# One core: the same 773 operations of an attention and token-mixing kernel in a newly solved order

## The chip, the cores and the metric

The kernel runs on one core of a Trainium2 chip. The metric is the device time of one execution in microseconds (us), the median of several runs.

## What is computed

Eight sequences of 576 tokens go through sliding-window attention with linear biases (8 heads of 64, window 128) and then, as 512 channels, through a token-mixing block. Inputs and output are fp32.

```python
scores = scale * np.matmul(q, k.transpose(0, 1, 3, 2))
mask = (rel >= 0) & (rel < window)
scores = np.where(mask, scores + bias[None], -1000000000.0)
attn = softmax(scores)
x = np.matmul(attn, v)                      # then heads side by side: [8, 576, 512]
...
wq = x @ w_q; wk = x @ w_k                  # 512 -> 64
W_tok = scale * np.einsum('bsd,btd->bst', wq, wk)
mixed = np.einsum('bst,btd->bsd', W_tok, x)
out = np.maximum(mixed, 0.0) @ w_out
```

## The kernel before

The kernel is built of 773 named operations. Each is declared once with `add` (its name, what it waits for, what it emits) and then emitted in the order of one long string, `ORDER`. One word of it is `name:engine`, and for TensorE also a PSUM place and a number of fillers:

```python
for word in ORDER.split():
    name, eng, *rest = word.split(":")
    ...
        op.bank = tuple(int(c) for c in rest[0])
        op.fill = int(rest[1]) if len(rest) > 1 else 0
```

Engines are P (TensorE), A (ScalarE), V (VectorE), G (GpSimd) and S (SyncE). Each engine runs its own words strictly in the order of the string, and waits at a word until what it depends on is done. PSUM is four pairs of banks; `:2` takes pair 2, `:21` its second bank. An operation that writes a place waits until the place's last content was evicted. `TW0.0:P:0:12` runs twelve products of a zero tile (fillers) ahead of TW0.0; they keep TensorE busy and compute nothing.

The names, with the batch as the first number:

- Loads, all issued by GpSimd: Lq, Lk, Lv and Lt (the last 64 tokens of q or k), Lwq, Lwk, Lwo (the weights). They cast fp32 to 16 bits. FQ0 and FQ1 load the first queries through SyncE, and CQ0 and CQ1 cast them. For batches 0 to 3 a q or k load takes four heads at once (256 KB in the tile); for batches 4 to 7 it takes 128 tokens (128 KB), like a v load.
- Constants: zerop, pads, zeros, ones0 to ones4 (memsets), iota, dist, mask, ident, idh, perm, bias, biasl.
- Attention: TW, TN and TT transpose q and k on TensorE (line 217), and ETW, ETN and ETT evict them. QK makes the scores of one block of keys and four heads, EXP evicts them with an exponential (ScalarE, line 604), MUL multiplies by the exponentiated bias and mask (VectorE, line 611). PV multiplies with v; its output also carries the row sums. X divides by them (VectorE, lines 649 and 650).
- Mixing: XT transposes x and EXT evicts it; WQ and WK are the two projections, G multiplies the second by x, MX mixes the tokens, RM is the relu, OUT the last product. EWQ, EWK, EG and EO evict. DO stores a block of 128 tokens, on GpSimd or SyncE.

All products go through one helper (line 214) and all loads through another (line 220), stores through line 223, so the profile's lines are those of helpers.

Loads are paced in the order in which they are emitted: each has a price in us, and a load waits until so many before it have landed that at most `AHEAD = 6.0` us of loads are under way. HOLD takes note of a load (the fourth from the end); the first SyncE store emitted behind HOLD waits for it. Stores emitted before HOLD do not wait for loads.

An eviction may run on ScalarE or VectorE; EXP is always ScalarE's, MUL and X always VectorE's.

Of the kernel before, what the change touches and what calls it, by code (L numbers as in the profile page):

```python
# [45 lines left out]
X0.0:V ETW1.1.0:A Lv0.4:G PV0.2:P:1 ETW1.1.1:A Lk2.1:G MUL0.3.0:V PV0.1:P:2 EXP0.3.1:A  # L46
X0.2:V Lk2.0:G QK1.2.1:P:0 EXP1.2.1:A QK1.1.1:P:3 MUL0.3.1:V Lq2.1:G TW1.0:P:1:1 X0.1:V
EXP1.1.1:A Lq2.0:G PV0.3:P:0 ETW1.0.0:A MUL1.1.1:V Lwq:G QK1.3.1:P:2 ETW1.0.1:A X0.3:V
PV0.4:P:3 EXP1.3.1:A QK1.0.1:P:1 X0.4:V Lv1.0:G XT0.0:P:0 EXP1.0.1:A EXT0.0:V Lv1.1:G
XT0.2:P:20:2 QK1.2.0:P:3 QK1.0.0:P:1 EXT0.2:A MUL1.0.1:V EXP1.2.0:A XT0.1:P:0 Lwk:G  # L50
QK1.1.0:P:2 MUL1.3.1:V EXP1.0.0:A EXT0.1:V Lv1.2:G TW2.1:P:3 MUL1.2.0:V EXP1.1.0:A Lv1.3:G
MUL1.2.1:V QK1.3.0:P:0 ETW2.1.1:A TW2.0:P:1 MUL1.0.0:V Lt1.2:G ETW2.1.0:A wqq:V EXP1.3.0:A
Lv1.4:G MUL1.1.0:V WQ0.0:P:20 ETW2.0.0:V PV1.0:P:3 Lt1.3:G ETW2.0.1:A WQ0.1:P:21 X1.0:V
EWQ0.0:A Lt1.1:G QK2.1.1:P:0 EWQ0.1:A QK2.0.0:P:1 Lwo.0:G PV1.1:P:2 MUL1.3.0:V EXP2.0.0:A
WK0:P:30 Lt1.0:G X1.1:V EXP2.1.1:A WQ0.2:P:31 PV1.2:P:1 Lk3.0:G EWQ0.2:V QK2.1.0:P:2 EWK0:A
ones4:G X1.2:V PV1.3:P:0 EXP2.1.0:A QK2.0.1:P:3 Lq3.0:G X1.3:V PV1.4:P:1 EXP2.0.1:A
# [6 lines left out]
RM1.1:V Lv2.3:G PV2.0:P:0 RM1.3:A ETW3.0.0:V OUT0.0:P:20 RM1.2:A X2.0:V Lq4.0:G EO0.1:A
OUT0.2:P:10 EO0.0:A MUL2.1.0:V QK3.0.0:P:3 MUL2.3.1:V Lq4.1:G QK3.1.0:P:0 EO0.2:A PV2.1:P:2
MUL2.3.0:V EXP3.0.0:A Lv3.0:G OUT1.0:P:11 X2.1:V EXP3.1.0:A Lq4.2:G PV2.2:P:3 MUL3.0.0:V
TW3.1:P:2 EO1.0:A Lk4.3:G MUL3.1.0:V X2.2:V QK3.2.0:P:0 ETW3.1.0:A Lk4.1:G PV2.4:P:1
EXP3.2.0:A ETW3.1.1:V OUT0.3:P:20 Lk4.0:G X2.4:V QK3.2.1:P:3 Lk4.2:G QK3.0.1:P:0 EO0.3:V
EXP3.2.1:A PV2.3:P:1 Lq4.3:G OUT1.3:P:21 EXP3.0.1:A X2.3:V Lv3.1:G WQ1.2:P:20 QK3.3.1:P:3
EWQ1.2:A EO1.3:V QK3.3.0:P:1 EXP3.3.1:A XT2.1:P:0 Lt2.3:G MUL3.2.1:V OUT1.2:P:20 Lv3.2:G
EXP3.3.0:A EXT2.1:V XT2.2:P:21 XT2.0:P:3 MUL3.0.1:V TN4.0.0:P:0 Lv3.4:G EXT2.2:A EXT2.0:A  # L70
MX1.2:P:1 WQ2.1:P:21 ETN4.0.0:V Lv3.3:G RM1.4:A QK3.1.1:P:3 MUL3.2.0:V EWQ2.1:A TN4.1.0:P:1
EXP3.1.1:A PV3.0:P:0 Lt2.0:G MUL3.3.1:V OUT1.4:P:21 Lv4.0:G X3.0:V ETN4.1.0:A TN4.0.1:P:3
EO1.2:A TN4.1.1:P:1 MUL3.1.1:V Lq5.3:G QK4.0.1:P:0 ETN4.0.1:A WK2:P:20 EO1.4:V ETN4.1.1:A
Lt2.2:G PV3.1:P:3 EXP4.0.1:A MUL3.3.0:V Lq5.2:G QK4.0.0:P:1 X3.1:V WQ2.0:P:21 EXP4.0.0:A
# [6 lines left out]
MUL4.1.1:V OUT2.1:P:21 Lq6.1:G X4.0:V ETN5.0.0:A Lk6.0:G TN5.1.0:P:0 EO2.3:A XT3.1:P:3
MUL4.3.0:V ETN5.1.0:A QK4.3.1:P:1 OUT2.2:P:20 Lv5.0:G EXP4.3.1:A EXT3.1:V MUL4.2.1:V Lt3.0:G
QK5.0.0:P:0 EO2.1:A QK5.0.1:P:3 MUL4.3.1:V EXP5.0.0:A PV4.1:P:1 Lk5.2:G EO2.2:V WK3:P:21
EXP5.0.1:A Lv5.1:G X4.1:V PV4.2:P:0 WQ3.1:P:20 Lk6.1:G EWK3:A X4.2:V QK5.1.0:P:3 EWQ3.1:A
QK5.1.1:P:1 EXP5.1.0:A PV4.3:P:2 Lv5.2:G MUL5.0.1:V PV4.4:P:0 EXP5.1.1:A X4.3:V Lq6.2:G
WQ2.2:P:30 G3:P:31 X4.4:V EWQ2.2:A Lq6.0:G XT4.1:P:2 EG3:A XT4.0:P:1 EXT4.1:A TN5.1.1:P:3
EXT4.0:V Lq7.0:G MX3.1:P:0 ETN5.1.1:A MX3.0:P:2 RM3.3:V OUT2.0:P:10 RM3.2:A Lk6.3:G RM3.1:V
RM3.0:A XT4.2:P:11 TN6.1.0:P:3 Lt3.2:G MUL5.0.0:V QK5.3.0:P:0 EXT4.2:A EO2.0:A QK5.3.1:P:2
ETN6.1.0:V Lv5.3:G OUT3.0:P:11 EXP5.3.1:A MUL5.1.1:V Lq6.3:G PV5.0:P:3 EXP5.3.0:A MUL5.1.0:V
OUT3.2:P:10 Lt3.1:G X5.0:V EO3.0:A WK4:P:20 Lk6.2:G EO3.2:A MUL5.3.1:V QK5.2.1:P:0  # L90
TN6.0.0:P:3 EWK4:A MX2.2:P:1 EXP5.2.1:A Lt3.3:G OUT3.1:P:21 ETN6.0.0:V Lk7.0:G RM2.4:V
PV5.1:P:3 MUL5.2.1:V EO3.1:A QK6.0.1:P:0 Lq7.1:G QK5.2.0:P:1 X5.1:V EXP6.0.1:A G4:P:20
Lv5.4:G MUL5.3.0:V WQ3.2:P:21 WQ4.0:P:30 EXP5.2.0:A Lk7.1:G EWQ3.2:V WQ4.1:P:31 EG4:V
EWQ4.0:V MX3.2:P:0 TN6.0.1:P:2 EWQ4.1:A Lk7.3:G TN6.1.1:P:1 RM3.4:V ETN6.0.1:A XT5.0:P:3
ETN6.1.1:V TT3:P:0 Lv6.2:G EXT5.0:A QK6.1.1:P:2 MUL5.2.0:V MX4.0:P:1 ETT6:A MX4.1:P:3
EXP6.1.1:A Lv7.3:G RM4.0:V OUT3.4:P:00 RM4.1:V RM4.3:A Lv6.1:G PV5.3:P:2 RM4.2:A MUL6.0.1:V
QK6.0.0:P:3 EO3.4:A Lv6.0:G PV5.2:P:1 X5.3:V ETT7:A OUT4.2:P:00 EXP6.0.0:A Lq7.2:G X5.2:V
QK6.1.0:P:2 Lq7.3:G QK6.2.1:P:3 MUL6.0.0:V EXP6.1.0:A TN7.1.0:P:1 OUT4.3:P:01 EO4.2:V
DO3.4:G EXP6.2.1:A ETN7.1.0:V PV5.4:P:2 MUL6.1.1:V QK6.3.0:P:1 EO4.3:A Lk7.2:G TN7.0.0:P:3
X5.4:V EXP6.3.0:A OUT4.1:P:00 Lv6.3:G MUL6.1.0:V ETN7.0.0:A QK6.3.1:P:2 XT5.1:P:1 MUL6.3.0:V  # L100
DO0.0:G EXP6.3.1:A QK6.2.0:P:3 OUT3.3:P:01 EO4.1:V Lv7.1:G EXT5.1:A MUL6.2.1:V PV6.0:P:2
EXP6.2.0:A DO2.2:G OUT4.0:P:00 X6.0:V Lv6.4:G EO3.3:A WQ5.1:P:10 MUL6.2.0:V EO4.0:A DO0.1:G
XT5.2:P:11 TN7.0.1:P:3 TN7.1.1:P:2 EWQ5.1:A EXT5.2:V QK7.0.0:P:0 ETN7.0.1:V DO2.3:G
ETN7.1.1:A PV6.2:P:1 MUL6.3.1:V EXP7.0.0:A DO1.0:G WQ5.0:P:30 X6.2:V PV6.1:P:2 Lv7.4:G
# [2 lines left out]
DO0.3:G QK7.3.1:P:3 X6.3:V G5:P:20 EXP7.3.1:A DO4.2:G XT6.0:P:0 EG5:V DO1.2:G XT6.1:P:1
EXT6.0:A XT6.2:P:21 QK7.0.1:P:3 EXT6.1:V EXT6.2:A Lv7.2:G EXP7.0.1:A MX5.1:P:0 MX4.2:P:2
WQ6.0:P:10 RM5.3:V DO3.0:G WK6:P:11 RM5.1:A MUL7.3.1:V RM4.4:A WQ5.2:P:30 DO1.4:G
QK7.2.1:P:0 EWQ5.2:A MUL7.0.0:V MX5.0:P:2 EWK6:A QK7.3.0:P:3 EWQ6.0:V RM5.0:A G6:P:11  # L110
RM5.2:V DO3.2:G EXP7.3.0:A WQ6.1:P:10 MUL7.1.0:V DO2.0:G OUT5.2:P:20 EG6:A EWQ6.1:V
EXP7.2.1:A MUL7.1.1:V OUT5.3:P:21 MUL7.3.0:V EO5.2:A MX6.1:P:1 MUL7.2.0:V MX5.2:P:3
MX6.0:P:0 EO5.3:A OUT5.1:P:20 RM5.4:V RM6.1:A MUL7.0.1:V RM6.3:A PV7.4:P:3 MUL7.2.1:V
RM6.2:A PV7.1:P:1 EO5.1:A X7.4:V OUT5.0:P:21 RM6.0:A DO5.1:G X7.1:V PV7.0:P:3 PV7.3:P:0
EO5.0:A X7.0:V WQ6.2:P:20 PV7.2:P:1 DO5.0:S OUT6.2:P:21 X7.3:V DO2.1:S OUT6.1:P:30 DO1.3:S
X7.2:V EO6.2:A EWQ6.2:A XT7.2:P:31 XT7.0:P:0 DO6.2:S EO6.1:V EXT7.2:A XT7.1:P:1 MX6.2:P:2
# [793 lines left out]
```

## Time and profile before

| | |
|---|---|
| Median of 3 runs | 138.8 us (138.38, 138.8, 142.11) |
| Span of the profiled execution, first to last instruction | 137.4 us |
| Median less that span | 1.4 us |
| Mean granted TensorE clock in the span | 0.983 |
| Data moved by DMA | 24.86 MB |
| Matmuls | 2364, of which 28 fillers |

The profile shows one execution. Its own time is the span and what lies around it; no separate time is listed for it, so the 1.4 us to the median stand for that. Times within the profile count from the first instruction. In the tables by stretches each row gives the stretch, its length, for each engine the busy time and, in brackets, the number of instructions, then the granted TensorE clock (1 is full), the summed share of the DMA queues and GB/s. The matmuls overlap, so that a mean duration is longer than the distance between two starts.

### The profile page before, as it was taken

How to read it: one execution, taken by the hardware profiler on the slowest of the kernel's cores; microseconds unless marked ns; L12 is line 12 of the kernel's file. 1: busy time of each engine (PE TensorE's matmuls, PEld its weight loads, DVE VectorE, ACT ScalarE, POOL GpSimd, SP SyncE). 2: the span in 40 equal slices, each digit the busy share in tenths (PEclk: the TensorE clock that was granted, in tenths of full speed). 3: DMA queues.
4: the chain of work that ended last, by engine and by line, in shares of the span. 5: the costliest groups of instructions: out<-in, count | busy, mean ns of one | idle time of the engine just before them, and what ended most of it. 6: DMA issues, size and time to landing. Idle time of an engine off the chain costs nothing.

```text
span 137.4 us, 5570 instructions
## 1 busy us (share of the span) xinstructions
PE 127.2 (93%) x2364; PEld 83.5 (61%) x2364; DVE 112.0 (82%) x236; ACT 113.8 (83%) x187; POOL 105.3 (77%) x170
## 2 busy tenths in 40 slices
...
GB/s 131 162 155 166 158 169 174 181 137 138 135 180 143 163 155 152 149 140 130 143 141 147 149 142 146 140 135 150 198 258 268 342 328 21 115 357 339 329 299 172
DMA packets 92680, 24.86 MB, mean 181 GB/s; under 512 B 80240, under 2 KB 89200, under 8 KB 92656
## 3 DMA queue, kind: packets, MB, share of 16 engines
...
q14 instruction: 6, 0.05, 0.1%
...
## 4 chain that ended last, share of the span: by engine, by line
PE 72%; ACT 8%; DMA 5%; POOL 5%; issue 3%; DVE 2%; POOLq 0%; DVEq 0%
PE pair L214 62%; PE pair L217 10%; DMA natw<-in_k_dram 5%; ACT pt L604 5%; POOL natt L220 2%; POOL natw L220 2%; ACT qkT L492 2%; DVE x L650 1%; DVE xtl L650 1%; DVE xT L237 1%; DVE inv L649 0%; ACT xT L235 0%; ACT osb L229 0%; ACT wqT L229 0%; POOL wm L293 0%
## 5 line engine op out<-in xcount | busy, mean ns | idle before, releaser
L604 ACT ACTIVATE pt<-pair 128x1024 f16<-128x1024 f32 x64 | 63.3, 1038 | 6.0 <-PE pair L214 5.8
L220 POOL DMA_DIRECT2D vt<-in_v_dram x40 | 36.5, 968 | 1.2 <-DMA natw<-in_k_dram 0.8
L611 DVE TENSOR_TENSOR pt<-pt,bias 128x1024 f16<-128x1024 f16 x48 | 32.2, 684 | 1.4 <-ACT pt L604 1.3
L214 PE MATMUL pair<-wout_sb,rm 128*128 128x512 f16 x128 | 32.0, 380 | 0.1
L223 POOL DMA_DIRECT2D out_dram<-natw x19 | 10.6, 566 | 19.5 <-DVE natw L231 10.9
L214 PEld LDWEIGHTS <-pt 128*128 128x128 f16 x576 | 21.2, 98 | 5.5 <-issue 2.2
L214 PE MATMUL pair<-qkT 64*128 64x256 f16 (+3 forms) x352 | 23.8, 247 | 0.4 <-ACT pt L604 0.3
L214 PE MATMUL pair<-vt,pt 128*128 128x65 f16 x576 | 23.8, 194 | 0.1
L220 POOL DMA_DIRECT2D natw<-in_k_dram x24 | 22.9, 993 | 1.2 <-POOLq L894 0.8
L220 POOL DMA_DIRECT2D natw<-in_q_dram x23 | 21.5, 989 | 2.0 <-DMA natw<-in_k_dram 0.7
L650 DVE TENSOR_TENSOR x<-pair,inv 128x512 f16<-128x512 f32 x32 | 22.1, 692 | 1.1
L214 PEld LDWEIGHTS <-rm 128*128 128x128 f16 x128 | 10.8, 97 | 10.9 <-issue 0.9
L214 PEld LDWEIGHTS <-qkT 64*128 64x128 f16 x352 | 11.9, 96 | 7.7 <-issue 3.9
L229 ACT COPY natw<-pair 128x512 f32<-128x512 f32 x24 | 14.1, 607 | 2.2 <-PE pair L214 2.1
L217 PEld LDWEIGHTS <-natw 128*64 128x64 f16 (+1 forms) x512 | 12.8, 103 | 4.8 <-issue 1.9
L214 PE MATMUL pair<-fill 128*128 128x512 f16 x28 | 10.4, 506 | 1.2 <-DVE fill L348 1.2
L750 ACT ACTIVATE rm<-pair 128x512 f16<-128x512 f32 x20 | 11.4, 611 | 0.0
L611 DVE TENSOR_TENSOR pt<-pt,biasl 128x1024 f16<-128x1024 f16 x16 | 10.9, 683 | 0.0
L217 PE MATMUL pair<-permh,natw 128*64 128x128 f16 x256 | 9.1, 223 | 1.8 <-DMA natw<-in_k_dram 1.4
L649 DVE RECIPROCAL inv<-pair 128x8 f32<-128x8 f32 (+1 forms) x40 | 8.1, 203 | 3.1 <-PE pair L214 2.3
L214 PE MATMUL pair<-xT,wqq_sb 128*128 128x256 f16 x64 | 9.3, 273 | 0.4 <-ACT qkT L492 0.4
L752 DVE TENSOR_SCALAR rm<-pair 128x512 f16<-128x512 f32 x12 | 7.9, 684 | 1.6 <-PE pair L214 1.6
...
## 6 DMA issues: line engine op xcount, KB each, us to landing
...
```

The source lines that it names most:

```text
L214: hold(nc.tensor.matmul(*a, **k))
L217: hold(nc.tensor.transpose(*a))
L220: hold(nc.gpsimd.dma_start(**k))
L223: i = (nc.gpsimd if eng == "POOL" else nc.sync).dma_start(**k)
L229: hold(nc.scalar.copy(out_ap, in_ap))
L492: hold(nc.scalar.copy(dst, src))
L604: nc.scalar.activation(out=pt[:, 0:1024], in_=two(s.bank).rearrange("p e c -> p (e c)"), func=AF.Exp, scale=SCALE)
L611: nc.vector.tensor_tensor(out=pt[:, 0:1024], in0=pt[:, 0:1024], in1=bt, op=ALU.mult)
L649: nc.vector.reciprocal(out=inv[r], in_=pxv[r, :, :, 64])
L650: nc.vector.tensor_tensor(out=x[r].rearrange("p (g h d) -> p g h d", g=2, h=4), in0=pxv[r, :, :, 0:64], in1=inv[r].unsqueeze(3).broadcast_ ...
L750: hold(nc.scalar.activation(out=out_ap, in_=in_ap, func=AF.Relu, scale=WSCALE))
L752: hold(nc.vector.tensor_scalar(out=out_ap, in0=in_ap, scalar1=0.0, scalar2=WSCALE, op0=ALU.max, op1=ALU.mult))
```

## The change

Only the string `ORDER` changes. The operations, their sizes and their dependencies stay. The order on all five engines, the engine of the evictions and of some constants and stores, and the PSUM place of each TensorE operation were solved anew by annealing, and TensorE's work was then pulled forward.

What differs, counted in the two strings: 28 fillers become 10, all ahead of TW0.0. 42 evictions go from VectorE to ScalarE and 41 the other way; the two casts CQ0 and CQ1 change places. zerop, pads and four of the five `ones` are set by VectorE (before: zerop, pads and three of the `ones` by GpSimd). GpSimd stores 13 blocks instead of 18, SyncE 23 instead of 18. HOLD stands at the very end, so no store waits for it. On TensorE, QK0.3.0 and QK0.3.1 come ahead of TW1.1, attention as a rule comes earlier and OUT later. Of the loads, most of batch 4's and 5's q and k come ahead of batch 4's v.

The diff, cut to the stretches that matter here:

```diff
-FQ1:S ones1:V FQ0:S Lk0.0:G ones0:V iota:G Lq0.1:G dist:V mask:G Lk0.1:G bias1:A ident:G
-CQ0:V CQ1:A Lt0.2:G zeros:V bias0:A idh:V Lt0.1:G perm:V TW0.0:P:0:12 Lt0.0:G biasl0:V
-Lq1.1:G ETW0.0.1:A ETW0.0.0:V Lt0.3:G QK0.2.0:P:1:5 Lk1.1:G QK0.1.0:P:2 EXP0.2.0:A Lv0.0:G
-TW0.1:P:0:1 EXP0.1.0:A Lv0.2:G QK0.0.0:P:3 ETW0.1.1:V ETW0.1.0:A zerop:G MUL0.1.0:V
-EXP0.0.0:A QK0.2.1:P:1:3 QK0.0.1:P:2 QK0.1.1:P:0 MUL0.0.0:V Lv0.1:G EXP0.1.1:A TT0:P:3
-biasl1:V Lk1.0:G EXP0.2.1:A MUL0.2.0:V Lq1.0:G TW1.1:P:0:2 EXP0.0.1:A MUL0.2.1:V pads:G
-ETT0:A MUL0.0.1:V QK0.3.0:P:1:2 ETT1:V EXP0.3.0:A Lv0.3:G PV0.0:P:2 MUL0.1.1:V QK0.3.1:P:3
...
-EXP4.2.1:A XT3.0:P:2 EG2:V Lk5.1:G OUT1.1:P:31 EXT3.0:V EXP4.1.0:A MUL4.2.0:V Lk5.3:G
-XT3.2:P:30 MX2.1:P:0 MX2.0:P:2 EO1.1:A EXT3.2:V RM2.1:V WQ3.0:P:10 Lv4.4:G RM2.3:A PV3.3:P:3
...
-EWQ4.2:V DO3.3:G PV6.4:P:2 EXP7.1.0:A EWK5:V QK7.2.0:P:0 DO1.1:G X6.4:V PV6.3:P:1 EXP7.2.0:A
...
+zerop:V FQ1:S FQ0:S pads:V Lk0.0:G iota:G ones2:V dist:V Lk0.1:G ident:G Lq0.1:G mask:G perm:V
+idh:V CQ1:V CQ0:A TW0.0:P:0:10 ETW0.0.0:V bias1:A bias0:A Lt0.2:G ones0:V Lt0.1:G Lt0.0:G
+Lt0.3:G Lq1.1:G ones1:G Lk1.1:G Lv0.0:G Lv0.1:G ETW0.0.1:A QK0.2.0:P:0 QK0.0.0:P:1 EXP0.2.0:A
+EXP0.0.0:A Lq1.0:G Lk1.0:G Lv0.2:G Lv0.3:G QK0.1.0:P:2 Lk2.1:G Lv0.4:G Lq2.1:G TW0.1:P:3 Lwq:G
...
+Lq4.3:G Lq4.2:G Lq4.0:G Lk4.3:G Lk4.2:G Lv3.1:G Lv3.4:G Lv3.2:G Lt2.3:G QK0.3.1:P:1 EXP0.3.1:A
+Lv3.3:G Lt2.1:G Lt2.2:G QK0.3.0:P:3 EXP0.3.0:A MUL0.1.1:V MUL0.3.1:V TW1.1:P:0 Lq5.3:G Lk5.3:G
+Lq5.1:G Lk5.1:G Lk5.0:G ETW1.1.0:A ETW1.1.1:A PV0.0:P:2 X0.0:V PV0.1:P:3 X0.1:V MUL0.3.0:V
...
+XT0.0:P:3 EXT0.0:A Lv4.1:G Lv4.0:G Lv4.2:G Lv4.3:G TW1.0:P:0 ETW1.0.1:A PV0.2:P:3 EXP1.2.1:A
...
+Lv6.4:G Lk7.2:G PV3.2:P:0 X3.2:V QK4.1.1:P:2 Lk7.3:G EXP4.1.1:A PV3.3:P:1 X3.3:V Lv6.2:G
...
+DO2.1:S EWK4:V X5.1:V PV5.0:P:3 X5.0:V MUL5.2.1:V MX3.2:P:2 TN6.1.1:P:1 RM3.4:A G4:P:01 EG4:V
...
+DO7.3:S OUT7.1:P:20 EO7.1:V DO7.1:S OUT7.2:P:01 EO7.2:A DO7.2:S HOLD:S
```

More of the change, by code (lines that the diff above doesn't have):

```diff
@@ L45 @@
-ETT0:A MUL0.0.1:V QK0.3.0:P:1:2 ETT1:V EXP0.3.0:A Lv0.3:G PV0.0:P:2 MUL0.1.1:V QK0.3.1:P:3
[L46 to L56, printed above, removed]
@@ L63 @@
[L63 to L74, printed above, removed]
@@ L81 @@
[L81 to L104, printed above, removed]
@@ L105 @@
-EWQ5.0:A QK7.1.1:P:0 QK7.1.0:P:3 X6.1:V Lv7.0:G EXP7.1.1:A WQ4.2:P:10 WK5:P:11 HOLD:S
-EWQ4.2:V DO3.3:G PV6.4:P:2 EXP7.1.0:A EWK5:V QK7.2.0:P:0 DO1.1:G X6.4:V PV6.3:P:1 EXP7.2.0:A
[L107 to L116, printed above, removed]
@@ new lines @@
+Lk3.1:G Lq3.1:G Lv2.0:G Lv2.1:G Lv2.2:G EXP0.1.1:A Lq3.0:G Lk3.0:G Lt2.0:G Lv2.3:G Lwo.0:G
+Lv2.4:G Lq4.1:G Lwo.3:G Lwo.1:G Lwo.2:G Lk4.0:G EXP0.0.1:A MUL0.0.1:V ETT1:V Lv3.0:G Lk4.1:G
+Lq4.3:G Lq4.2:G Lq4.0:G Lk4.3:G Lk4.2:G Lv3.1:G Lv3.4:G Lv3.2:G Lt2.3:G QK0.3.1:P:1 EXP0.3.1:A
+Lv3.3:G Lt2.1:G Lt2.2:G QK0.3.0:P:3 EXP0.3.0:A MUL0.1.1:V MUL0.3.1:V TW1.1:P:0 Lq5.3:G Lk5.3:G
+Lq5.1:G Lk5.1:G Lk5.0:G ETW1.1.0:A ETW1.1.1:A PV0.0:P:2 X0.0:V PV0.1:P:3 X0.1:V MUL0.3.0:V
+QK1.1.1:P:0 EXP1.1.1:A Lq5.0:G MUL1.1.1:V QK1.0.1:P:2 EXP1.0.1:A MUL1.0.1:V QK1.2.1:P:1 Lq5.2:G
@@ new lines @@
+XT0.0:P:3 EXT0.0:A Lv4.1:G Lv4.0:G Lv4.2:G Lv4.3:G TW1.0:P:0 ETW1.0.1:A PV0.2:P:3 EXP1.2.1:A
+ETW1.0.0:V QK1.0.0:P:0 Lk6.0:G Lk5.2:G Lk6.1:G X0.2:V Lq6.0:G Lq6.1:G PV0.3:P:2 X0.3:V
+EXP1.0.0:A MUL1.0.0:V QK1.3.1:P:3 EXP1.3.1:A PV0.4:P:1 X0.4:V XT0.1:P:2 EXT0.1:A QK1.2.0:P:0
+EXP1.2.0:A Lq6.2:G Lv5.0:G Lv4.4:G TW2.1:P:3 ETW2.1.1:A QK1.1.0:P:1 XT0.2:P:20 EXT0.2:A
+EXP1.1.0:A wqq:V MUL1.2.1:V WQ0.1:P:00 ETW2.1.0:V QK2.0.1:P:3 QK1.3.0:P:2 EXP1.3.0:A WQ0.0:P:01
+Lq6.3:G MUL1.2.0:V EWQ0.1:V WQ0.2:P:00 EWQ0.2:A Lv5.1:G Lk7.1:G EXP2.0.1:A MUL1.1.0:V Lt3.1:G
@@ new lines @@
+Lk7.0:G Lk6.2:G EWQ0.0:V MUL1.3.1:V TW2.0:P:1 Lv5.2:G MUL1.3.0:V QK2.1.1:P:0 PV1.0:P:2 X1.0:V
+PV1.1:P:3 X1.1:V Lk6.3:G ETW2.0.0:A ETW2.0.1:A EXP2.1.1:A QK2.0.0:P:1 EXP2.0.0:A PV1.2:P:2
+X1.2:V QK2.2.1:P:0 EXP2.2.1:A PV1.4:P:3 X1.4:V Lt3.2:G QK2.2.0:P:1 EXP2.2.0:A PV1.3:P:2 X1.3:V
+TT1:P:0 ETT2:A ETT3:A MUL2.2.0:V XT1.2:P:30 WK0:P:31 EWK0:A EXT1.2:V XT1.0:P:2 EXT1.0:A
+XT1.1:P:0 EXT1.1:A G0:P:31 EG0:A QK2.3.0:P:2 EXP2.3.0:A MUL2.1.1:V MUL2.0.1:V MUL2.2.1:V
+MUL2.0.0:V QK2.1.0:P:1 QK2.3.1:P:0 EXP2.1.0:A MUL2.3.0:V EXP2.3.1:A TW3.1:P:3 MUL2.1.0:V
@@ new lines @@
+WK1:P:20 WQ1.2:P:21 WQ1.0:P:10 WQ1.1:P:11 ETW3.1.0:V EWQ1.0:V PV2.1:P:0 X2.1:V EWQ1.2:A
+ETW3.1.1:A QK3.0.1:P:3 EWK1:A EWQ1.1:A PV2.0:P:2 X2.0:V EXP3.0.1:A MX0.1:P:1 RM0.3:A RM0.1:A
+PV2.2:P:0 X2.2:V QK3.2.1:P:3 TW3.0:P:2 MX0.2:P:0 EXP3.2.1:A XT2.0:P:1 ETW3.0.1:A ETW3.0.0:A
+MUL2.3.1:V RM0.4:V QK3.1.1:P:3 EXP3.1.1:A PV2.3:P:0 EXT2.0:V QK3.1.0:P:2 Lv5.3:G Lt3.0:G Lv5.4:G
+Lt3.3:G EXP3.1.0:A Lv6.0:G PV2.4:P:1 X2.3:V Lq7.0:G Lq7.1:G Lv7.2:G G1:P:30 EG1:A MX0.0:P:0
+RM0.0:A Lq7.3:G Lq7.2:G QK3.0.0:P:2 X2.4:V XT2.1:P:1 EXP3.0.0:A RM0.2:V QK3.3.0:P:3 WQ2.0:P:00
```

65 lines of the change are left out of this document (49 added, 16 removed).

## The prediction

> **What bounds the kernel now.** I read the page first, then the table by stretches, the chain of work that ended last, and the timelines of TensorE, GpSimd and ScalarE. The page: TensorE is busy 93% of the span, the two engines that empty PSUM about 82% each, GpSimd, which issues every load, 77%.
>
> ```profile
> span 137.4 us, 5570 instructions
> PE 127.2 (93%) x2364; PEld 83.5 (61%) x2364; DVE 112.0 (82%) x236; ACT 113.8 (83%) x187; POOL 105.3 (77%) x170
> ```
>
> The table by stretches of 10 us (engine columns in page order, then granted clock and DMA):
>
> ```profile
> 10.00:20.00 10.00, 7.69 (x129) 4.56 (x124) 5.97 (x12) 6.73 (x10) 9.43 (x23) 0.84 1.77 165
> 20.00:30.00 10.00, 9.32 (x243) 7.51 (x244) 9.47 (x19) 9.99 (x15) 7.40 (x10) 0.99 1.59 165
> 30.00:40.00 10.00, 9.25 (x218) 7.06 (x213) 9.04 (x22) 9.20 (x16) 9.71 (x30) 1.00 1.54 147
> ...
> 70.00:80.00 10.00, 10.00 (x250) 7.14 (x249) 9.62 (x20) 9.56 (x17) 10.00 (x13) 1.00 2.27 146
> ...
> 120.00:130.00 10.00, 10.00 (x120) 5.53 (x118) 5.97 (x13) 5.33 (x13) 0.54 (x1) 1.00 0.94 340
> ```
>
> From 40 us on TensorE has no gap, so there the end is the sum of its work. Before 40 us it waits: for ScalarE (9.99 of 10 in 20:30) and, ahead of that, for loads. GpSimd is full at 70:80 too, issuing loads. The chain agrees:
>
> ```profile
> 9.12 7.13 DMA natw<-in_k_dram
> ...
> 16.29 1.03 PE pair L217 x24
> ...
> 122.33 10.14 PE pair L214 x84
> 132.47 0.02 issue
> 132.49 0.59 ACT osb L229
> ```
>
> TW1.1 stands at the head of TensorE's queue until Lk1.1 lands at 16.25, and ScalarE pays for it:
>
> ```profile
> 18.87 1.02 ACT L604 ACTIVATE pt<-pair 128x1024 f16<-128x1024 f32 x1 [3.18 <-PE pair L214]
> ```
>
> The last product ends at 132.47; eviction, store and end take the 4.9 us to 137.4.
>
> **The change, part by part.** The operations are the same 773; only order, engine and bank differ.
>
> *Fillers.* 28 become 10.
>
> ```profile
> L214 PE MATMUL pair<-fill 128*128 128x512 f16 x28 | 10.4, 506 | 1.2 <-DVE fill L348 1.2
> ```
>
> All stand before 27 us, where TensorE waits anyway: credit 0. What they cover is the clock (a rival below).
>
> *Evictions.* 42 go to ScalarE, 41 to VectorE; priced at their groups' means, ScalarE's sum grows by 0.1 us. VectorE gains 2.8 us of constant setting (memsets from GpSimd), most of it before the first product. Cost 0 under the wait for the first loads; about 1.2 us of it lies beside the ScalarE-bound units before 16 us, which bounds it.
>
> *TensorE's own sum.* Priced op by op at the usual distance between starts, both orders give 113.0 us from the first transpose to the last product. Six more changes between whole-array and half-array products are in it; one costs about 0.1 us: OUT to OUT is 127.97 - 127.10 = 0.87, OUT to a half-array op 67.00 - 66.03 = 0.97.
>
> ```profile
> 66.03 1.04 PE L214 MATMUL pair<-wout_sb,rm 128*128 128x512 f16 x4
> 67.00 0.22 PE L217 MATMUL pair<-identh,xtl 64*128 64x64 f16 x1
> ...
> 127.10 1.04 PE L214 MATMUL pair<-wout_sb,rm 128*128 128x512 f16 x4
> 127.97 1.03 PE L214 MATMUL pair<-wout_sb,rmt 128*128 128x512 f16 x4
> ```
>
> So a gain can come only from waits, some 13 us (132.47 - 6.4 - 113.0), nearly all before 40 us.
>
> *The early waits.* QK0.3.0 and QK0.3.1 now go ahead of TW1.1, so ScalarE has two units to do while Lk1.1 lands: most of the 3.18 us goes. Evictions then run some 2 us earlier. What is late next is the loads: the new order brings attention forward and puts OUT products back, so a given load is wanted with less TensorE work ahead of it.
>
> *The loads.* GpSimd's pace does not change. These are its issues of Lv3.2, Lv3.4 and Lv3.3, of Lv4.0, of Lk6.1, and TensorE's PV3.4, PV3.3, PV4.0 and the stretch with TN6.1.0:
>
> ```profile
> 54.60 2.52 POOL L220 DMA_DIRECT2D vt<-in_v_dram  x3
> 57.02 0.79 POOL L220 DMA_DIRECT2D natt<-in_q_dram  x1
> 57.70 0.99 POOL L220 DMA_DIRECT2D vt<-in_v_dram  x1
> 58.57 0.99 POOL L220 DMA_DIRECT2D natw<-in_q_dram  x1
> ...
> 74.31 1.15 POOL L220 DMA_DIRECT2D natw<-in_k_dram  x1
> 75.18 1.16 POOL L220 DMA_DIRECT2D vt<-in_v_dram  x1
> DMA to landing us min/median/max: 4.0/5.1/7.1
> ```
> ```profile
> 63.42 0.66 PE L214 MATMUL pair<-vt,pt 128*128 128x65 f16 x16
> 68.14 0.65 PE L214 MATMUL pair<-vt,pt 128*128 128x65 f16 x16
> 70.82 0.43 PE L214 MATMUL pair<-vt,pt 128*128 128x65 f16 x8
> 81.64 0.36 PE L217 MATMUL pair<-identh,natw 64*128 64x64 f16 x12
> ```
>
> One v or token load per 0.87 us (58.57 - 57.70), one tail load per 0.68 (57.70 - 57.02); issue to landing 4.0 to 5.1 in this stretch, I take 4.6. For three loads I ask: when does it land, and how much TensorE work is left from its user on?
>
> PV3.3. The new order puts behind it the stretch 63.42 to 68.14 (PV3.4 to WQ3.0, 4.7 less 0.2 of waiting) and OUT1.0, 1.2, 1.3, 1.4 (3.5); it puts WQ2.2 (0.1) ahead of it and has more of those changes there (0.6): 7.2. Work left: 132.47 - 68.14 + 7.2 = 71.5. Lv3.3 has the same loads ahead of it as before and Lt2.0 (0.7): issued at 56.2 + 0.7, landing 61.5. End 133.0.
>
> PV4.0. Behind it go OUT1.1, 1.2, 1.4, 2.3 and XT3.2 (3.6), ahead come OUT2.2, two QK, XT3.1, TN5.1.0 and WQ2.2 (2.0), the changes make 0.5: 1.1 more left, 61.65 + 1.1 = 62.8. Lv4.0 now queues behind ten further loads, eight at 0.87 and two at 0.68: issue 57.7 + 8.3 = 66.0, landing 70.6. End 133.4.
>
> TN6.1.0. 6.8 us more work left: 132.47 - 81.6 + 6.8 = 57.7. Lk6.1 overtakes three v or token loads and two short ones (4.0): issue 70.3, landing 74.9 to 75.4. End 132.6 to 133.1.
>
> Against them stands that GpSimd loses 3.8 us of memsets ahead of these loads (5.0 leave it, 1.2 come). But it idles later for landings:
>
> ```profile
> 11.62 1.00 POOL L336 MEMSET pt<- 128x64 f16 x10
> 15.25 1.01 POOL L340 MEMSET xtl<- 128x512 f16 x2
> ...
> 44.97 0.88 POOL L220 DMA_DIRECT2D natw<-in_q_dram  x1 [0.64 <-issue]
> 46.11 0.88 POOL L220 DMA_DIRECT2D natw<-in_q_dram  x1 [0.27 <-DMA natw<-in_k_dram]
> ```
>
> So up to 46 us the transfers, not the issues, set its pace, and the memsets were free. Bounds 0 and 3.8; I take 0.4, near the low end by that row. The last product then ends at 133.0, 0.5 later than now. The waits after PV4.0 are in the 61.65 already.
>
> *Stores.* Five fewer on GpSimd, five more on SyncE, whose first now waits for EO2.1 (about 87 us) instead of standing behind HOLD and EO5.0. HOLD itself cost nothing: SyncE waited for EO5.0 long after it. The three last stores:
>
> ```profile
> 119.03 11.73 SPq L223 DMA_DIRECT2D out_dram<-natw  x17
> 131.37 2.06 SPq L223 DMA_DIRECT2D out_dram<-osb  x3
> DMA to landing us min/median/max: 2.1/4.3/5.2
> ```
>
> 17 stores in 11.7 us leave a backlog, so that the last, issued at 133.1, ends at 136.4, 3.3 us. Most stores go out earlier in the new order; its backlog is shorter and the last takes between 2.1 and 3.3: I take 2.6, a gain of 0.7. Stores among the last loads cost nothing: PV7.1 comes 10 us after Lv7.1.
>
> *Sum.* Against the profiled span: +0.5 - 0.7 = -0.2. The median of the runs is 138.8, 1.4 above that span, so 138.6. Two per cent, 2.8 us, is about what a measurement of this kernel tells from no change.
>
> **Rivals.** *The loads come sooner* (faster). If the 3.8 us of freed issue slots do bring the loads forward by 2.5 us or more, the end follows ScalarE's early gain: 3.18 less about 1 that comes back at TW1.1 and TW1.0, so 2.2; with the stores 2.9. 135.9. For it: GpSimd's full stretches. Against: the idle rows at 45 us.
>
> *Hand-overs without slack* (slower). In the old order the eviction that each TensorE op waits for has more and more room from 40 us on; counted by prefix sums, the new one keeps ScalarE and VectorE level with TensorE until about 70 us. The place is the run of QK, EXP and PV of batches 3 to 5. The price: in 20:30 and 30:40, where ScalarE is 9.99 and 9.20 full, TensorE loses 0.68 and 0.75 of 10 us. Kept over 40 to 80 us that is 2.9: 141.5. It decides from a loss of 0.3 per 10 us on. Against: a load-bound lag leaves the evictions some 2 us of room.
>
> *The clock* (slower). Without the 18 fillers TensorE is emptier until 20 us.
>
> ```profile
> 10.00:13.40 3.40, 2.83 (x52) 1.59 (x46) 2.18 (x4) 3.31 (x5) 3.40 (x13) 1.00 1.44 154
> 13.40:16.80 3.40, 1.67 (x35) 1.04 (x37) 2.96 (x7) 2.30 (x4) 3.05 (x8) 1.00 2.13 160
> 16.80:20.20 3.40, 3.38 (x54) 2.12 (x49) 1.03 (x3) 1.33 (x2) 2.98 (x4) 0.51 1.73 177
> 20.20:23.60 3.40, 3.09 (x75) 2.30 (x73) 3.06 (x7) 3.40 (x5) 2.03 (x3) 0.99 1.41 169
> ```
>
> A stretch 1.67 of 3.40 busy was followed by one at 0.51 of the clock, and that, full, by the full clock. I expect one or two more such stretches after 10 us. Each costs 1.7 us where TensorE isn't waiting, and some 2 us are free before the loads bind. Three more in the dense part: 3 x 1.7 - 2 = 3.1, 141.7.
> The Trainium skill (TensorE: Matmul & The Clock Gate, "Part 4: PE-mode transpose") says that transposes do not count as busy for this gate. By that the early TW stretches would count as idle and this rival would gain; the row 13.40:16.80, mostly transposes and waiting, agrees but does not separate the two.
>
> *The change does not do what it says.* Counted in the orders, the work ahead of QK7.3.0 is 92.1 us against 92.5: not pulled forward as a whole. What moves is which work comes first. This is within the forecast.
>
> **How the numbers follow.** Forecast 138.6, chance 0.52, its own range 137.2 to 140.4; loads sooner 0.16 (135.9); hand-overs 0.22 (141.5); clock 0.10 (141.7). Below 136.0: over half of the second (0.09) and the forecast's lower tail (0.07): 0.16. Above 141.6: half of the hand-overs and of the clock (0.11 and 0.06) and the forecast's upper tail (0.05): 0.22. Within: 0.62. The range goes from 135.6, the lower rival with a little more, to 142.2, the upper two with a little more.
>
> **What would show it.** Right: ScalarE's wait before its seventh or eighth unit falls from 3.18 to under 1; a stretch at half clock before 17 us; TensorE at 10.00 no longer from 40 us on, but waits between 45 and 72 us whose releaser is a load of v, q or k; the last store under 3 us. Wrong: waits in 45 to 80 us released by ScalarE or VectorE (hand-overs); no waits there and an end before 131 (loads sooner); half clock after 25 us.

## The result, and the profile after

| | before | after |
|---|---|---|
| Median | 138.9 us (4 runs) | 143.65 us (142.48, 143.33, 143.97, 144.56) |
| Ratio to before, 95% interval | | 1.0345 [1.0275, 1.0416] |
| Span of the profiled execution | 137.4 us | 140.7 us |

Slower by 4.8 us. The prediction, 138.6 us with 135.6 to 142.2, was wrong, and its range missed. Medians here are over all executions, ratios leave out those more than 1.5% above the fastest of the same kernel. The profiled execution of after is the fastest of the four (142.48), so its 3.3 us over the span before are less than the loss in the median. First the page, then the table by stretches (engine columns in page order, then granted clock, DMA share, GB/s), and under it two rows of the kernel before:

```profile
span 140.7 us, 5535 instructions
PE 123.1 (87%) x2346; PEld 83.2 (59%) x2346; DVE 114.6 (81%) x261; ACT 113.7 (81%) x188; POOL 98.5 (70%) x139
```
```profile
10.00:20.00 10.00, 6.38 (x162) 5.00 (x157) 9.30 (x32) 9.51 (x14) 7.92 (x12) 1.00 1.61 155
...
70.00:80.00 10.00, 9.27 (x211) 6.73 (x205) 8.31 (x18) 8.91 (x16) 10.00 (x13) 1.00 2.33 150
80.00:90.00 10.00, 10.00 (x202) 6.94 (x200) 9.61 (x19) 9.36 (x17) 10.00 (x14) 1.00 2.06 151
90.00:100.00 10.00, 9.20 (x183) 5.48 (x180) 8.74 (x18) 8.90 (x16) 8.60 (x12) 1.00 2.25 166
100.00:110.00 10.00, 8.77 (x182) 6.20 (x181) 8.16 (x17) 6.95 (x12) 5.34 (x9) 1.00 1.23 275
```
```profile
90.00:100.00 10.00, 9.99 (x200) 6.24 (x192) 9.76 (x19) 9.76 (x16) 9.86 (x14) 1.00 2.05 168
100.00:110.00 10.00, 9.82 (x228) 7.38 (x227) 9.09 (x20) 9.40 (x16) 8.90 (x15) 1.00 1.31 287
```

TensorE did 127.2 us of busy time before and does 123.1 now (18 fillers fewer), in a longer span. Before it was 10.00, 9.99 and 9.82 busy in 70:80, 90:100 and 100:110; now it is 9.27, 9.20 and 8.77, and ScalarE and VectorE are not full there. The table of waits says for whom (us in total, times, longest):

```profile
PE pair L210 <- ACT qkT L488: 3.2, 4, 1.5
...
PE pair L210 <- ACT qkT L231: 2.6, 3, 1.2
...
PE pair L213 <- DMA natw<-in_q_dram: 1.7, 2, 1.0
...
PE pair L210 <- DMA vt<-in_v_dram: 0.8, 2, 0.7
```

L488 are the evictions ETW, before 40 us. L231 with tile qkT are ETN and ETT: three waits, one in each thin stretch. The timeline of TensorE at the three places, and under it that of ScalarE (start, duration, operation, and in brackets the idle time before it):

```profile
75.02 0.27 PE L210 MATMUL pair<-qkT 64*128 64x256 f16 x2
75.87 0.28 PE L210 MATMUL pair<-qkT 64*128 64x256 f16 x2 [0.57 <-ACT qkT L231]
...
93.50 0.39 PE L210 MATMUL pair<-qkT 64*128 64x256 f16 x4 [0.80 <-ACT qkT L231]
...
102.05 0.29 PE L210 MATMUL pair<-qkT 64*128 64x256 f16 x2
103.57 0.28 PE L210 MATMUL pair<-qkT 64*128 64x256 f16 x2 [1.23 <-ACT qkT L231]
```
```profile
75.23 0.59 ACT L231 COPY qkT<-pair 128x512 f32<-128x512 f32 x1
...
92.80 0.65 ACT L231 COPY qkT<-pair 128x256 f32<-128x256 f32 x2
...
102.92 0.59 ACT L231 COPY qkT<-pair 128x512 f32<-128x512 f32 x1
```

The first is QK5.1.0, cut in two: two of its four matmuls at 75.02, the other two at 75.87, when ETN5.1.1 (75.23 + 0.59 = 75.82) has ended. QK6.1.0 starts at 93.50, after ETT7 and ETT6 (to 93.45). QK7.0.0 is cut like the first and waits for ETN7.1.1 (to 103.51). But none of the three reads what it waits for: QK5.1.0 takes keys 128 to 255 of its qkT tile, ETN5.1.1 writes keys 256 to 511; ETT6 writes tokens 512 to 575, of which QK6.1.0 reads none; QK7.0.0 takes keys 0 to 127. From start to start the three gaps are 0.84, 0.99 and 1.50 us; the same pairs of matmuls stand 0.11, 0.03 and 0.09 us apart in a_cols below, so the three cost 0.74, 0.96 and 1.41: 3.1. (The expectations count 0.84, 0.97 and 1.50, 3.3 in all.)

### The profile page after: what moved, and what is told of

Same layout as the page of the kernel before. It is cut to its first block, busy times and chain, and to the rows that moved or that the text cites. A ratio compares the mean times of both kernels' runs of the same rounds, so it can differ in the third digit from the quotient of the medians.

```text
span 140.7 us, 5535 instructions
## 1 busy us (share of the span) xinstructions
PE 123.1 (87%) x2346; PEld 83.2 (59%) x2346; DVE 114.6 (81%) x261; ACT 113.7 (81%) x188; POOL 98.5 (70%) x139
## 4 chain that ended last, share of the span: by engine, by line
PE 40%; POOL 25%; DMA 21%; ACT 5%; issue 4%; DVE 1%; POOLq 0%; ACTq 0%
PE pair L210 36%; POOL natw L216 13%; DMA natw<-in_q_dram 8%; DMA vt<-in_v_dram 7%; POOL vt L216 7%; DMA natw<-in_k_dram 5%; PE pair L213 4%; POOL natt L216 3%; ACT pt L600 3%; ACT qkT L231 1%; POOL wout_sb L216 1%; DVE pt L607 0%; ACT osb L225 0%; POOL vt L319 0%; POOL wm L289 0%
## 5 line engine op out<-in xcount | busy, mean ns | idle before, releaser
L216 POOL DMA_DIRECT2D vt<-in_v_dram x40 | 37.0, 955 | 4.9 <-DMA natw<-in_q_dram 2.3
L607 DVE TENSOR_TENSOR pt<-pt,bias 128x1024 f16<-128x1024 f16 x48 | 31.6, 685 | 0.5 <-ACT pt L600 0.2
L216 POOL DMA_DIRECT2D natw<-in_k_dram x24 | 22.4, 993 | 2.0 <-POOLq L890 0.8
L646 DVE TENSOR_TENSOR x<-pair,inv 128x512 f16<-128x512 f32 x32 | 22.1, 692 | 1.3 <-DVE inv L645 0.2
L219 POOL DMA_DIRECT2D out_dram<-natw x15 | 8.2, 553 | 18.0 <-ACT natw L225 13.2
L210 PEld LDWEIGHTS <-qkT 64*128 64x128 f16 x352 | 12.2, 94 | 13.1 <-issue 5.5
L748 DVE TENSOR_SCALAR rm<-pair 128x512 f16<-128x512 f32 x15 | 9.9, 685 | 1.3 <-PE pair L210 1.2
L746 ACT ACTIVATE rm<-pair 128x512 f16<-128x512 f32 x17 | 9.6, 610 | 0.3 <-PE pair L210 0.3
L231 ACT COPY qkT<-pair 128x512 f32<-128x512 f32 (+1 forms) x16 | 8.4, 547 | 0.6 <-PE pair L213 0.4
```

What stands on the lines that cost most here:

```text
L210: hold(nc.tensor.matmul(*a, **k))
L216: hold(nc.gpsimd.dma_start(**k))
L219: i = (nc.gpsimd if eng == "POOL" else nc.sync).dma_start(**k)
L231: hold(nc.scalar.copy(out_ap.bitcast(FP32), in_ap.bitcast(FP32)))
L607: nc.vector.tensor_tensor(out=pt[:, 0:1024], in0=pt[:, 0:1024], in1=bt, op=ALU.mult)
L646: nc.vector.tensor_tensor(out=x[r].rearrange("p (g h d) -> p g h d", g=2, h=4), in0=pxv[r, :, :, 0:64], in1=inv[r].unsqueeze(3).broadcast_ ...
```

## The experiments

**The false waits.** The program tells the evictions of one qkT tile apart from each other, but not a QK from evictions of other columns, so the QK waits for all that stand ahead of it in the string. Which matmuls wait fits a comparison of ranges, from the first column of an access to its last: the first two of QK5.1.0 and of QK7.0.0 read columns that lie ahead of all that the eviction writes, and run; their other two, and all four of QK6.1.0, read between its first and its last column. No run tests this reading. Theory: that is the loss. Rivals: loads that land late, and the clock without the 18 fillers. a_cols and b_cols let a QK wait only for the evictions that it reads and for those that empty its own PSUM pair, in the new and in the old order. By the same lines an eviction no longer waits for QKs of its batch that stand ahead of it and read other columns.

```diff
 def apart(op):
...
+    if op.name.startswith("QK"):
+        keep += freed.get(op.bank[0], [])
+    for f in op.frees:
+        freed.setdefault(f.bank[0], []).extend(held)
...
-        s = add(f"QK{b}.{g}.{u}", pe(0.228), need, em, banks=2, mode=1)
+        s = add(f"QK{b}.{g}.{u}", pe(0.228), need, em, banks=2, mode=1, group=f"q{b}")
```

> The kernel after, in the same order, but a QK no longer waits for evictions that write other columns of its qkT tile (it waits for those it reads and for its own PSUM pair). False waits: QK5.1.0, QK6.1.0 and QK7.0.0 lose gaps of 0.84, 0.97 and 1.50 us in the trace after, 3.3 us in all, and nothing else is late there: span 137.4 in a run at full clock, 2.5 to 3.3 us less than the kernel after in the median. Loads bind: the loads of batches 6 and 7 take the gaps over, 0 to 1 us less. Clock: the gaps had let the gate close or not; the time stays within 1 us and the mean granted clock falls.

> The same edit in the kernel before. False waits: TensorE has no gap there after 40 us, the evictions that it would wait for stand behind the QK in the string; within 0.4 us of the kernel before. If the edit gives 1 us or more here too, the gain in the kernel after says nothing on the change.

Measured: a_cols 140.45 us, 1.0081 [1.0040, 1.0122] of before, 3.2 us less than after. b_cols 138.53 us, 0.9951 [0.9911, 0.9991]. The edit takes 3.2 us from the new order and 0.5 from the old one. The timeline of TensorE in a_cols shows the three QKs whole and without a bracket:

```profile
span 138.9 us, 5536 instructions
```
```profile
76.30 0.38 PE L210 MATMUL pair<-qkT 64*128 64x256 f16 x4
...
93.08 0.38 PE L210 MATMUL pair<-qkT 64*128 64x256 f16 x4
...
101.66 0.40 PE L210 MATMUL pair<-qkT 64*128 64x256 f16 x4
```

a_string gets there by the string alone: four words move, and the order on each engine stays as it was.

```diff
-TN5.1.1:P:2 ETN5.1.1:A QK5.1.0:P:1
+TN5.1.1:P:2 QK5.1.0:P:1 ETN5.1.1:A
-TT3:P:2 ETT7:A ETT6:A X5.3:V QK6.1.0:P:1
+TT3:P:2 X5.3:V QK6.1.0:P:1 ETT7:A ETT6:A
-TN7.1.1:P:2 ETN7.1.1:A QK7.0.0:P:1
+TN7.1.1:P:2 QK7.0.0:P:1 ETN7.1.1:A
```

> The kernel after with four words moved in the string: ETN5.1.1 behind QK5.1.0, ETT7 and ETT6 behind QK6.1.0, ETN7.1.1 behind QK7.0.0. The order on each engine stays as it was; the helper's code too. False waits: the three gaps of 0.84, 0.97 and 1.50 us go, unless the eviction now waits for the QK's reads (it does so for 0.4 us at most, ScalarE has nothing urgent behind it): 2.5 to 3.2 us less than the kernel after, as a_cols. If the gaps come from a late ScalarE and not from the place in the string: no change.

Measured: 140.93 us, 1.0124 [1.0063, 1.0184], 2.7 us less than after. So the place of a word among those of other engines costs time, though no engine's own order changes. The two edits are different and give the same within their intervals.

**The clock.** a_fill28 puts the 28 fillers of before back at the same operations (`QK0.2.0:P:0` becomes `QK0.2.0:P:0:5` and so on); b_fill10 takes 18 from the kernel before.

> The kernel after with the 28 fillers of the kernel before at the same operations (12 on TW0.0, 5 on QK0.2.0, 3 on QK0.2.1, 2 each on TW1.1, QK0.3.0 and XT0.2, 1 each on TW0.1 and TW1.0). Clock: the mean granted clock rises from 0.95-0.96 to 0.98 or more in most executions and the median falls by 1 to 2 us. False waits or loads alone: no change in the clock, the time within 0.5 us, or up to 1.5 us more where a filler stands in a place that no longer waits (18 more at 0.22 to 0.5 us each).

> The kernel before with 10 fillers, all on TW0.0, as in the kernel after. Clock: the granted clock falls to 0.95-0.96 in most executions, 1 to 2 us more. Otherwise: within 0.4 us of the kernel before, since the fillers stand where TensorE waits anyway.

Measured: a_fill28 143.51 us, 1.0331 [1.0277, 1.0385], at mean clocks of 0.991 to 0.998, where the four executions of after had 0.948 to 0.996. b_fill10 138.51 us, 0.9979 [0.9940, 1.0017], with the clock down to 0.963. The rows of the granted clock in 40 slices, a_fill28 first, then b_fill10:

```profile
PEclk9999999999999999999999999999999999999996
```
```profile
PEclk9965868999999999999999999999999999999999
```

The fillers do hold the clock, and neither median follows it: the 4.8 us do not come from leaving 18 fillers out, and the theory falls. Both runs change fillers and clock together, though, and fillers take time too: in the trace of a_fill28 TW1.0 starts at 22.3 us, at full clock, against 20.0 in after and 21.8 in a_cols, which has half-clock stretches. Execution by execution the kernel before is shorter at a higher clock: of those that ran beside these and count in the ratio, the 16 at a mean clock of 0.989 or more took 137.9 to 139.4 us, the seven below 139.0 to 139.9. The twelve of a_cols show no such tie (139.5 at 0.966, 140.5 at 0.991). Whether in the kernel before the clock or the waiting is the cause stays open.

**The loads.** After a_cols the new order is still 1.9 us behind b_cols (1.0081 less 0.9951, 1.3% with some 0.6 either way). Its TensorE waits for loads in the stretch where the forecast saw them, here at TN5.0.0 (68.94) and PV4.0 (71.64):

```profile
68.94 0.41 PE L213 MATMUL pair<-identh,natw 64*128 64x64 f16 x16 [0.53 <-DMA natw<-in_q_dram]
...
71.64 0.42 PE L210 MATMUL pair<-vt,pt 128*128 128x65 f16 x8 [0.26 <-DMA vt<-in_v_dram]
```

a_nok and b_nok are a_cols and b_cols without the 16 words Lk4.0 to Lk7.3; the k transposes of these batches read the tile of q in their place:

```diff
-                           tp(dst[:, hp, n, :], tok(b, j, 2 * m + n)[h, P * hp:P * hp + P], identh[h, h])
+                           tp(dst[:, hp, n, :], tok(b, 0, 2 * m + n)[h, P * hp:P * hp + P], identh[h, h])
```

> a_cols without the 16 k loads of batches 4 to 7; their k transposes read q's tile, so the scores of these batches are q with q. Loads bind: TensorE's lag (start less work ahead) is 12.2 us from 46 to 57 us in a_cols and rises to 13.6 at PV4.0, where Lv4.0 lands; without the k loads it stays at 10.5 to 12.3 to the end (14.3 now): 1.5 to 2.5 us less than a_cols, 138 to 139 in the median. Hand-overs (evictions late): lag and time within 0.5 us of a_cols.

> b_cols without the 16 k loads of batches 4 to 7, in the same way. Loads bind only in the new order: from 45 us on each load of the kernel before lands 1.7 us or more ahead of its user, so the time stays within 0.4 us of b_cols (138.5). If it falls by 1 us or more too, the k loads cost something that the order has no part in.

Measured: a_nok 140.64 us, 1.0104 [1.0036, 1.0171], no gain on a_cols. b_nok 137.78 us, 0.9904 [0.9864, 0.9944], 0.75 less than b_cols, more than the 0.4 expected. So late landings after 60 us alone do not hold the new order back. In a_nok TensorE's lag at 50 us (an operation's start, less the 6.4 us at which TensorE starts, less the work ahead of it) was that of a_cols, 12.0 and 12.2 us.

a_hold moves `HOLD:S` ahead of `DO2.1:S`; a_edf also sorts the loads from Lt2.0 on by TensorE's first use.

> a_cols with HOLD ahead of DO2.1, so that no SyncE store goes out before the fourth load from the end has landed (some 102 us). Stores among loads: Lq7.0 and what is behind it landed 7.1 us after issue in a_cols, right after the first two SyncE stores (87 us), against 4.5 us for the loads around; now 4.5 to 5, landing 2 us sooner (Lq7.0 at 91.2 to 92), and the small waits at TN7.0.0 and TN7.0.1 go: 0.3 to 0.6 us less than a_cols, less what the later stores cost at the end (0 to 0.7). Otherwise the late landings stay and nothing moves.

> a_hold with the loads from Lt2.0 on in the order in which TensorE wants them (so Lk5.3, Lv4.1, Lv3.4, Lt2.0 and Lq4.1 go back, Lv4.0 and Lq5.0 come forward). Loads: Lv4.0 lands 1.7 us sooner against TensorE's work, the waits at TN5.0.0 and PV4.0 (0.9 to 1.3 us together in a_cols and a_hold) go: 0.5 to 1.2 us less than a_cols. If a second limit stands as close (a_nok, without k loads, was not faster): 0 to 0.4 less.

Measured: a_hold 140.80 us, 1.0109 [1.0062, 1.0157]; a_edf 140.54 us, 1.0123 [1.0069, 1.0178]. Neither gains. Stores do delay loads: Lq7.0 landed 7.1 us after its issue in a_cols (86.7 to 93.8) and 4.2 in a_hold (86.9 to 91.0). But TN7.0.1 started at 97.3 against 97.2, so nothing that counted was waiting. In a_edf Lv4.0 landed sooner (69.9 against 71.5) and Lq6.1 later (79.1 against 77.4): the waits moved to TN6.1.0 and TN6.0.0 (0.55 and 0.60 us).

**The instructions.** In a_cols, a_hold, a_nok and a_string TensorE stops once near 38 us, after its 606th matmul, in the middle of G0, with all that G0 reads long there. The timeline of a_cols, and the row that names it in its table of waits:

```profile
37.56 0.63 PE L210 MATMUL pair<-x,wkn 128*64 128x256 f16 x8
39.73 0.30 PE L210 MATMUL pair<-xtl,wkn 128*64 128x256 f16 x2 [1.54 <-issue]
```
```profile
PE pair L210 <- issue: 1.5, 1, 1.5
```

The DMA records hold a queue of instructions, and in the window 37.1 to 38.1 one packet of it:

```profile
q8 instruction: 1, 0.02, 5.6%
```

It started at 37.17 and took 0.9 us; TensorE went on 1.7 us after its end. Such a packet (16 KB) comes once per 127 matmuls with their weight loads, and it comes while TensorE works in the block before. In after itself that packet ended 2.1 us after the 479th matmul and there was no stop; in a_cols, a_hold, a_nok and a_string it ended 3.9 to 4.7 us after it, and the block, dense with the short matmuls of TT1, XT1, WK0 and G0, takes 4.4. In a_fill28 and a second time in a_string the stop comes at the 733rd matmul, 127 on, in PV2.1 and PV2.2: it goes by the count, not by the operation. Two runs tested it: a_fillxt (`XT1.0:P:2` becomes `XT1.0:P:2:5`) and a_ahead3 (`AHEAD = 3.5`).

> a_cols with 5 fillers (1.1 us at full clock) ahead of XT1.0, in the stretch of TT1, XT1, WK0 and G0 with 127 matmuls in 4.3 us of work. In a_cols, a_hold, a_nok and a_string TensorE stands still for 0.7 to 1.5 us after its 606th matmul with nothing that it waits for in the program, and 1.3 to 1.5 us after the end of a packet of its instructions. Instructions come late: the fillers are done while it would stand still, the gap after the 606th matmul falls by about 1.1, to 0 to 0.5, and TensorE's start less work (fillers not counted) at 50 us stays at 11.2 to 12.3. Another cause: the gap stays and the lag at 50 us is 1 us more, 13 or above.

> a_cols with at most 3.5 us of loads under way in place of 6.0. Instructions queue behind loads: the packet that is asked for after the 479th matmul lands 1 to 2.5 us after it (3.9 to 4.7 in a_cols, a_hold, a_nok and a_string) and the gap after the 606th is gone. Otherwise it lands as late as before. The loads themselves may come later, and the time be up to 3 us more: only the gap and the packet count here.

The timeline of a_fillxt:

```profile
36.53 1.24 PE L210 MATMUL pair<-fill 128*128 128x512 f16 x5
37.70 0.72 PE L213 MATMUL pair<-identh,x 64*128 64x64 f16 x32
38.35 0.67 PE L210 MATMUL pair<-x,wkn 128*64 128x256 f16 x8
38.81 0.32 PE L210 MATMUL pair<-xtl,wkn 128*64 128x256 f16 x2
...
43.36 0.43 PE L210 MATMUL pair<-vt,pt 128*128 128x65 f16 x8
45.30 0.39 PE L210 MATMUL pair<-wqT,gs 64*128 64x512 f16 x2 [1.51 <-DVE x L651]
```

The stop in G0 is gone, as expected: 1.1 us of fillers were done in it. But the next packet was late too, and TensorE stops after its 733rd matmul and goes on 1.5 us after that packet's end. (The bracket names X2.0, which ended at 44.97; MX0.1, which starts there, doesn't read it, so I take this for the same kind of stop, but the row alone doesn't show it.) The lag at 50 us was 12.5, a little over the 12.3 expected; the time 140.16 us, 1.0123 [1.0070, 1.0177], that of a_cols: 1.1 us of fillers cost nothing that can be measured. In a_ahead3 the packet after the 479th matmul ended 3.0 us after it and that after the 606th 1.4 (4.2 in a_cols), and no stop is left at either. The first missed the expected 1 to 2.5 us, after itself had 2.1 with 6.0 us of loads under way, and a_nok17 below has 4.2 with 22 loads fewer; that the packets queue behind the loads is not shown. The kernel took 164.8 us: its TensorE waits for loads from 22 us on to 121 us.

**Both together.** a_nok17 and b_nok17 also leave out Lk1.0 to Lk3.1.

> a_cols without the k loads of batches 1 to 7 (22 of them); their k transposes read q's tile, so the scores of these batches are q with q. What is left of the loss after a_cols, 1.9 us against b_cols, comes from loads in two ways, late data (60 to 77 us) and TensorE's instructions queued behind loads (after the 606th or 733rd matmul): with less traffic from 17 us on both go, TensorE's start less work at 50 us is 10.0 to 11.3 (12.2 in a_cols) and the time within 0.5 us of b_nok17. Evictions without slack, which no load sets: the lag at 50 us stays near 12 and the time 1.4 us or more above b_nok17.

> b_cols in the same way without the k loads of batches 1 to 7. Its loads had slack from 45 us on, ahead of that less than 2 us: 0.5 to 1.5 us less than b_cols by fewer waits before 46 us; it is the partner of a_nok17, and only the difference between the two counts.

Measured: a_nok17 137.84 us, 0.9925 [0.9883, 0.9967]; b_nok17 136.65 us, 0.9861 [0.9778, 0.9944]. The lag of a_nok17 at 50 us fell to 9.8, below the 10.0 to 11.3 expected, and it gained 2.6 us on a_cols by the medians, 2.2 by the ratios. The two orders stand 0.9 us apart by the ratios (0.64%, with some 0.9% either way; 1.2 by the medians) where they stood 1.9: between the two expectations, and not settled by the times. The profiles differ by 1.0 us (spans 135.7 and 134.8), and the new order's has the stop in G0 still, its packet ending 4.2 us after the 479th matmul:

```profile
35.91 0.63 PE L209 MATMUL pair<-x,wkn 128*64 128x256 f16 x8
37.62 0.30 PE L209 MATMUL pair<-xtl,wkn 128*64 128x256 f16 x2 [1.08 <-issue]
```

**One part alone.** b_early takes the step on which the early gain of the forecast rested into b_cols:

```diff
-TW1.1:P:0:2 EXP0.0.1:A MUL0.2.1:V pads:G
-ETT0:A MUL0.0.1:V QK0.3.0:P:1:2 ETT1:V EXP0.3.0:A Lv0.3:G PV0.0:P:2 MUL0.1.1:V QK0.3.1:P:3
...
-EXP0.3.1:A
+ETT0:A EXP0.0.1:A MUL0.2.1:V ETT1:V MUL0.0.1:V
+QK0.3.0:P:1:2 QK0.3.1:P:3 EXP0.3.0:A EXP0.3.1:A TW1.1:P:0:2 pads:G Lv0.3:G PV0.0:P:2 MUL0.1.1:V
```

> b_cols with one part of the change alone: QK0.3.0 and QK0.3.1 ahead of TW1.1, EXP0.3.0 and EXP0.3.1 ahead of its evictions, ETT0 ahead of EXP0.0.1. Early gain: ScalarE does two units while Lk1.1 lands, TW1.0 starts some 1.2 us sooner than in b_cols (20.94). The loads of this order land 1.7 us or more ahead of their users from 45 us on, so most of it stays: 0.6 to 1.2 us less than b_cols, 137.3 to 137.9 in the median, below both kernels. Early loads bind (1 us of slack or less at 20 to 30 us): 0 to 0.3 less.

Measured: 138.71 us, 1.0017 [0.9985, 1.0049]: no gain. But this is no test of the early gain, which never came: TW1.0 started at 22.1, not at 19.7 (20.9 in b_cols), behind a TW1.1 at 16.98 (14.16 in b_cols), and ScalarE waited 1.50 and 1.37 us for TensorE at 18.94 and 21.38. b_cols itself shows more. It was 1.0 us ahead of the kernel before at QK3.0.0 (46.1 against 47.1), and then TensorE waited for a load of v:

```profile
51.00 0.64 PE L214 MATMUL pair<-vt,pt 128*128 128x65 f16 x16 [0.86 <-DMA vt<-in_v_dram]
```

That operation, PV2.4, starts at 50.98 in the kernel before, and TensorE's lag at 51 us was 11.1 us in b_early and b_cols. So the loads of the old order had no room there, against the expectation. No complete version beat b_cols, which is 0.5% faster than before.

## Why the prediction was wrong, point by point

- **The step that failed: "The waits after PV4.0 are in the 61.65 already."** It took the gaps of the old order for those of the new, and counted a wait only where an operation's declared dependencies have one. The new order stands three QKs behind evictions of their tile that they do not read. From the start of PV4.0 to the end of the last product the forecast had 62.8 us; it was 65.6 in after, and 62.5 in a_cols and 62.7 in a_string. In the median the false waits cost 3.2 us (a_cols) or 2.7 by moving four words (a_string), of 4.8 in all. In the old order QK7.0.0, for one, stands ahead of ETN7.1.1.
- *The loads.* The mechanism was right, the term too small. Lv4.0 landed at 70.24 (forecast 70.6, or 70.2 with the 0.4 taken off) and PV4.0 started there:

```profile
70.37 0.32 PE L210 MATMUL pair<-vt,pt 128*128 128x65 f16 x5 [0.16 <-DMA vt<-in_v_dram]
```

Without the false waits the last product ends at 133.3 (a_string) to 134.6 (a_edf), forecast 133.0, and the median of a_cols is 1.9 us over the 138.6. What the forecast had no row for is late instructions, and later landings in some executions (71.5 in a_cols). How the 1.9 us split between the two stays open; in a_string, with two stops before 46 us, PV4.0 still started at 70.64, right behind its load (70.42).
- *The early waits.* Right in the trace, with little worth in time. ScalarE's 3.18 us are gone, four units run in one piece:

```profile
13.60 3.84 ACT L600 ACTIVATE pt<-pair 128x1024 f16<-128x1024 f32 x4
```

But what is won early is used up at the loads: the trace of a_string is 1.45 us behind that of after at OUT0.1 (51.39 against 49.94) and 0.27 at PV4.0. The sum gave this gain nothing of its own, and rightly.
- *Fillers, credit 0:* right in the medians (b_fill10, a_fill28). The clock rival was wrong: half-clock stretches came before 25 us, in a_cols, a_string and a_hold, not in the dense part. They put TW1.0 at 21.1 to 21.8 us against 20.0 in after; in a_string 0.3 of that is left at PV4.0. By the Trainium skill (TensorE: Matmul & The Clock Gate, "Part 4: PE-mode transpose") that rival would have gained; these runs don't test the rule, since the medians did not follow the clock.
- *Stores.* The gain of 0.7 was 0.2. The last product's chain row ends at 135.98, 4.7 us ahead of the span's end (4.9 before):

```profile
125.85 10.13 PE pair L210 x82
```

"Stores among the last loads cost nothing" held: they cost landings, but no time (a_hold).
- *The hand-overs rival* named its sign (wait in 45 to 80 us released by ScalarE, at 75.87) and put it at 141.5. Its reason was another: the evictions were not late, TensorE waited for evictions that it did not need. Two of the three waits lie after 80 us. That its 141.5 is nearer to the 143.65 than the forecast is luck.
- *The 1.4 us* between span and median: in the runs since, an execution takes 1.8 us more than its span (140.67 against 138.9 in a_cols). By that the profiled execution before took 139.2, 0.4 over the median, and 1.8 less 0.4 is the 1.4 again. This term is no part of the miss.
- *The signs.* Three of the four for the forecast stood in the trace of after: ScalarE's wait, waits for loads of v (59.85 and 70.37), the last store in 2.9 us. The half clock before 17 us did not (1.00 in this execution), and the sign for the hand-overs stood beside them.
